# Windowed attention with an RWKV channel mix on one core: the second half of each early group's exponentials goes through GpSimd, one long ScalarE exponential and VectorE, and the written order of the opening is a new one

## The chip, the cores and the metric

The kernel runs on one core of one Trainium2 chip. The metric is device microseconds of one execution of the whole program, weights and inputs loaded from HBM, result written back to it. All data are float32 at the kernel's edges.

## The reference

Attention over 8 batches, 8 heads, 576 positions and 64 values per head, in which a position sees itself and the 63 before it; its output is the input `x` (512 columns) of an RWKV channel mix with a hidden width of 1024.

```python
scores = np.matmul(q, k.transpose(0, 1, 3, 2)) / np.sqrt(D)
mask = (rel >= 0) & (rel < 64)                 # rel = row - column
scores = np.where(mask, scores, -1e9)
scores = scores - np.max(scores, axis=-1, keepdims=True)
attn = np.exp(scores)
attn = attn / (np.sum(attn, axis=-1, keepdims=True) + 1e-09)
x = np.matmul(attn, v)                         # heads side by side: B, S, 512

x_prev = np.concatenate([zeros, x[:, :-1]], axis=1)
xk = mu_k * x + (1.0 - mu_k) * x_prev
xr = mu_r * x + (1.0 - mu_r) * x_prev
k = np.maximum(xk @ w_k, 0.0)                  # 512 x 1024
v = k * k @ w_v                                # 1024 x 512
r = 1.0 / (1.0 + np.exp(-(xr @ w_r)))          # 512 x 512
return r * v
```

## The kernel before

The 4608 positions are cut into nine units of 512. A unit's attention is done by groups: one group is a pair of heads over one unit, four groups to a unit, 36 groups. The first eight groups (two units), called whole, work on blocks of 128 key columns; the later ones work on narrower bands of 32 rows, and are turned by VectorE.

A whole group `g` goes through these steps. `whole_scores` (TensorE) fills two PSUM banks, one for each head, `h` = 0 and 1, from `qk`, the queries and keys of the group; the queries and keys of groups 2 and 3 lie in a buffer named `qks`. For each head, `soften` then makes four blocks of 128 columns. For each block, `least` (VectorE, with its read of an accumulator) writes the negated, masked scores to `pr` and their smallest to `nmax`, and `exp` (ScalarE, followed by a read of an accumulator) takes the exponential of the block, with `nmax` as its bias and the row sum as second output. When all eight blocks of both heads are done, `shares` (two short VectorE instructions) makes the reciprocals `rs`, and `scale`, once for each head and over 512 columns, multiplies `pr` by them on GpSimd or VectorE. `flip` transposes the four blocks of a head on TensorE against `ident`; a copy on ScalarE or VectorE brings them from PSUM to `pt`. `whole_values` (TensorE, needs `v`) multiplies, a copy brings the result to `xT`, and a few elementwise steps on ScalarE, GpSimd and VectorE mix it with the position before into `xm`. The products of `xm` with the weights follow.

The weights come in as raw blocks of 512 KB (`raw`, from `w_r`, `w_k`, `w_v`), and each half of a block is decoded once: a sign on ScalarE (`wt<-raw`), a clamp on GpSimd or VectorE (`wt<-wt`), then three VectorE steps that need a PSUM bank for a while and end in `whole`. The first products use `whole` in float32 (`xm,whole`); the later ones use `ws`, the weight split in two parts by a cast and a subtraction, three instructions for a product (`xs,ws` and `ks,ws`).

Each piece of work is recorded with a helper, so that nearly all instructions carry that helper's line, L160 before and L161 after. `ORDER` is a table that writes out, for each engine, the order of the first 1700 or so pieces by their numbers; a piece waits until all that it needs is done, and whatever stands behind it on its engine waits with it. `play` places the rest. The queue `SP` issues all the loads in the order of its own list. `values`, the counterpart of `whole_values` for the banded groups, begins every pair of groups with an instruction that fills TensorE's instruction stream with empty instructions up to a given place in a window of 128 instructions:

```python
            tc.keep_in_program_order(nc.tensor.addr_align(128, offset=ALIGN))
```

`ALIGN` is 102. The number of empty instructions that it makes depends on how many instructions of TensorE stand ahead of it.

Of the kernel before, what the change touches and what calls it, by code (L numbers as in the profile page):

```python
# [13 lines left out]
AF = mybir.ActivationFunctionType  # L14
ALU = mybir.AluOpType
PSUM = bass.MemoryType.PSUM

P = 128
# [5 lines left out]
G = 4  # L24
# [26 lines left out]
USTEPS = 40  # L51


PAIRED = 8

WHOLES = 8
# [12 lines left out]
FAR_LINK = 45  # L69

ALIGN = 102

RING = 8

# [1 line left out]

ORDER = {
# [11 lines left out]
    ),  # L89
    "DVE": (  # L90
# [13 lines left out]
    ),  # L104
    "ACT": (
# [12 lines left out]
    ),  # L118
    "POOL": (
# [4 lines left out]
    ),  # L124
# [8 lines left out]
    ),  # L133
}
# [7 lines left out]
def attn_rwkv_kernel(ctx, tc, qT, kT, v2, mu_k, mu_r, w_k, w_v, w_r, out):  # L142
    nc = tc.nc
# [18 lines left out]
    pe, dve, sca, pool, dma = (Engine(e) for e in (nc.tensor, nc.vector, nc.scalar, nc.gpsimd, nc.sync))  # L162
# [120 lines left out]
    def d1(n):  # L283
        return 65 + 1.04 * n
# [4 lines left out]
    def act_ns(n):  # L289
        return 5 + 0.92 * n  # L290
# [10 lines left out]
    engines = {"DVE": dve, "POOL": pool}  # L301

    def bank(*shape):
        return psum.tile([P, *shape], F32, name="bank")
# [78 lines left out]
    words, whole, pairs, rooms = {}, {}, {}, {}  # L383
# [177 lines left out]
            arrived["v", g] = [transfer(lambda e, x=x: load_whole(e, *x), 4 * P * P * (x[3] - x[2]), held["v", g], key=key)  # L561
                               for x in whole_loads[u]]

    banks, weights, sums, flipped = {}, {}, {}, {}
    xTs, got = {}, {}
    chain = {}

# [9 lines left out]
                          k[hr, k0:k0 + P], start=True, stop=True)  # L577

    def flip(g, h):
        ps = flipped[g, h] = bank(G, P)  # L580
        for e in range(G):
            pe.transpose(ps[:, e, :], weights[g, h][:, e, :], ident)
# [118 lines left out]
    def soften(g, h, p, own):  # L701
        u, _ = groups[g]
        key = p.key + 0.5
# [5 lines left out]
        rows = Hold("pr")  # L709
        if h == 0:  # L710
            chain[g, "sums"], chain[g, "exps"] = Hold("sums"), []
        exps, begin = chain[g, "exps"], None
        for o in range(G):
            def least(e, o=o):
                if o == 0:
                    pr = at.tile([P, G * P], F32, name="pr", bufs=4)
                    weights[g, h] = pr[:, :G * wide].rearrange("p (i k) -> p i k", k=wide)
                    if g not in sums:
                        sums[g] = [at.tile([P, 2, G], F32, name=nm, bufs=4) for nm in ("nmax", "sums", "rs")]
                if whole:  # L720
                    starts = [(u * UB + 2 * o + j) % NB for j in range(2)]
                    mask = masks[starts.index(0) if 0 in starts else None]
                else:
                    mask = banded[first.get(o)]
                dve.tensor_tensor_reduce(weights[g, h][:, o], banks[g][h][:, o], mask,
                                         scale=-SCALE, scalar=FAR, op0=ALU.add, op1=ALU.min,
                                         accum_out=sums[g][0][:, h, o:o + 1])

            def exp(e, o=o):
                pr = weights[g, h]  # L730
                sca.activation(pr[:, o], pr[:, o], AF.Exp, bias=sums[g][0][:, h, o:o + 1], scale=-1.0,
                               accum_out=sums[g][1][:, h, o:o + 1])

            takes = [rows, chain[g, "sums"]] if o == 0 else []
            q = Piece("DVE", key, 211 if whole else 180, least, [p, begin, chain.get("masks")], takes, own)
            begin = begin or q
            exps.append(Piece("ACT", key, 385 if whole else 356, exp, [q]))
            chain["least"] = q
        chain[g, h, "pr"] = rows
        if h == 0:  # L740
            return
# [346 lines left out]
```

## Time and profile before

| what | value |
|---|---|
| median of three runs | 624.54 us (624.25, 624.54, 627.5) |
| the profiled execution, its time | 623.52 us |
| the profiled execution, its span | 621.7 us |
| granted TensorE clock, mean | 0.999 of full speed |
| TensorE products, busy | 603.0 us, 97% of the span |
| VectorE, busy | 399.7 us, 64% |
| ScalarE, busy | 372.8 us, 60% |
| GpSimd, busy | 118.7 us, 19% |
| read from HBM, written to it | 45.09 MB, 9.44 MB |

The span runs from the first to the last instruction of the profiled execution; the time of the execution is 1.8 us longer. Busy shares are over the whole span, and PE stands for TensorE's products, PEld for its weight loads, DVE for VectorE, ACT for ScalarE, POOL for GpSimd, SP for the queue of the loads. A row of a timeline gives start and length in microseconds, and in brackets how long the engine was idle ahead of it and what ended that.

### The profile page before, as it was taken

The page shows a single profiled execution, that of the slowest core. Times are in us where ns is not written, and L with a number is a line of the kernel's source. Part 1 is how long each engine was busy: PE and PEld are TensorE (multiplying, and loading weights), DVE is VectorE, ACT ScalarE, POOL GpSimd, SP SyncE. Part 2 cuts the span into 40 slices and gives each one's busy share as a digit, 9 for nine tenths or more (in the row PEclk, how much of TensorE's full clock was granted, in tenths as well). Part 3 has the DMA queues.
Part 4 walks back from the last instruction along what each step waited for, and adds up shares of the span by engine and source line. Part 5 has one row for each costly group of instructions (what it writes and reads, how often), then busy time and mean ns, then how long its engine had stood idle before and what let it go on. Part 6 is the DMA issues. An engine that isn't in the chain of part 4 may idle for free.

```text
span 621.7 us, 18051 instructions
## 1 busy us (share of the span) xinstructions
PE 603.0 (97%) x7168; PEld 474.2 (76%) x7168; DVE 399.7 (64%) x1218; ACT 372.8 (60%) x1058; POOL 118.7 (19%) x189
## 2 busy tenths in 40 slices
PE   2999999989999999999999999999999999999997
PEld 2655478878888888888888888888888888888885
DVE  5999998766685468636872778276837684665211
ACT  5989975558356735763575448564757466734630
POOL 6551532311210122011300330023002200111000
PEclk9999999999999999999999999999999999999999
DMA  8995213313231223123222322133212231010001
GB/s 309 363 322 163 96 28 100 107 34 92 68 115 35 78 76 107 43 65 94 84 74 53 105 88 74 53 90 102 76 53 90 77 100 28 1 53 18 0 18 51
DMA packets 58866, 55.70 MB, mean 90 GB/s; under 512 B 10144, under 2 KB 52128, under 8 KB 58784
## 3 DMA queue, kind: packets, MB, share of 16 engines
q1 hardware_dynamic: 58784, 54.56, 28.2%
q8 instruction: 57, 0.93, 0.7%
q14 instruction: 25, 0.20, 0.1%
HBM read 45.09 MB, written 9.44 MB: 88 GB/s over the span
## 4 chain that ended last, share of the span: by engine, by line
PE 95%; DVE 2%; DMA 1%; issue 1%; SPq 0%; POOL 0%; ACT 0%; DVEq 0%
PE bank L160 95%; DMA raw<-w_r 1%; DVE pr L160 1%; SPq L160 0%; DVE bank L160 0%; DVE xm L160 0%; POOL pr L160 0%; DVE mu L160 0%; DVE r L160 0%; ACT wt L160 0%; POOL wt L160 0%; DVE whole L160 0%; DVE rs L160 0%; DVE nmax L160 0%; DVEq L160 0%
## 5 line engine op out<-in xcount | busy, mean ns | idle before, releaser
L160 PE MATMUL bank<-xs,ws 128*128 128x512 f32 x1152 | 273.0, 396 | 0.0
L160 PEld LDWEIGHTS bank<-xs,ws 128*128 128x128 f32 x1152 | 215.8, 188 | 51.2
L160 PE MATMUL bank<-ks,ws 128*128 128x512 f32 x864 | 206.2, 397 | 0.0
L160 PEld LDWEIGHTS bank<-ks,ws 128*128 128x128 f32 x864 | 161.4, 188 | 38.8 <-issue 0.5
L160 DVE TENSOR_TENSOR ks<-kf,ks 128x512 fp32r<-128x512 f32 x71 | 51.7, 730 | 105.1 <-ACT ks L160 105.1
L160 ACT ACTIVATE pr<-pr,nmax 128x96 f32<-128x96 f32 (+1 forms) x288 | 105.9, 371 | 10.1 <-DVE nmax L160 9.6
L160 ACT ACTIVATE kf<-bank 128x512 f32<-128x512 f32 x72 | 42.9, 598 | 64.9 <-PE bank L160 64.9
L160 POOL CAST ks<-kf 128x512 fp32r<-128x512 f32 x10 | 6.1, 610 | 266.3 <-ACT kf L160 266.3
L160 ACT COPY xT<-bank 128x256 f32<-128x256 f32 (+1 forms) x35 | 13.2, 419 | 72.1 <-PE bank L160 72.1
L160 ACT ACTIVATION_READ_ACCUMULATOR pr<-pr,nmax 128x1 f32 x288 | 54.6, 190 | 0.0
L160 DVE CUSTOM_DVE_ANT_0 pr<-bank,bands 128x96 f32<-128x96 f32 x224 | 42.6, 249 | 14.1 <-PE bank L160 14.1
L160 PEld LDWEIGHTS bank<-pt,v 32*64 32x64 f32 (+1 forms) x2912 | 39.2, 131 | 9.6 <-issue 7.5
L160 ACT ACTIVATE kf<-kf 128x512 f32<-128x512 f32 x71 | 44.7, 632 | 2.1
L160 PE MATMUL bank<-pt,v 32*64 32x64 f32 (+3 forms) x2912 | 42.1, 235 | 2.4 <-issue 2.0
L160 ACT ACTIVATE th<-bank 128x512 f32<-128x512 f32 x36 | 21.3, 592 | 38.0 <-PE bank L160 27.5
L160 DVE SCALAR_TENSOR_TENSOR r<-bank,r 128x512 f32<-128x512 f32 x36 | 24.5, 680 | 30.1 <-PE bank L160 30.1
L160 PE MATMUL bank<-xm,whole 128*128 128x512 f32 x96 | 42.4, 594 | 0.5 <-DVE xm L160 0.5
L160 ACT CAST ks<-kf 128x512 fp32r<-128x512 f32 x62 | 38.4, 620 | 2.5 <-POOL kf L160 0.7
L160 PE MATMUL bank<-qk 64*32 64x96 f32 (+1 forms) x1984 | 33.4, 256 | 6.6 <-DMA qk<-kT 6.6
L160 PEld LDWEIGHTS bank<-qk 64*32 64x32 f32 (+1 forms) x1984 | 28.6, 110 | 13.9 <-DMA qk<-qT 7.0
L160 ACT CAST xs<-d 128x512 fp32r<-128x512 f32 x51 | 30.6, 615 | 13.6 <-POOL d L160 11.5
L160 DVE TENSOR_TENSOR xs<-d,xs 128x512 fp32r<-128x512 f32 x57 | 36.4, 681 | 0.1
(82 smaller groups left out, 546.7 us busy)
## 6 DMA issues: line engine op xcount, KB each, us to landing
v<-v SPq DMA_DIRECT2D x116, 64.0 KB, 2.1
raw<-w_k SPq DMA_DIRECT2D x8, 512.0 KB, 7.1
raw<-w_v SPq DMA_DIRECT2D x8, 512.0 KB, 4.9
v<-v SPq DMA_DIRECT2D x112, 32.0 KB, 1.8
v<-v SPq DMA_DIRECT2D x11, 192.0 KB, 5.2
raw<-w_r SPq DMA_DIRECT2D x4, 512.0 KB, 6.5
outT<-r SPq DMA_DIRECT2D x8, 256.0 KB, 2.0
qk<-qT SPq DMA_DIRECT2D x8, 224.0 KB, 3.6
```

The lines of the kernel that those rows point to most:

```text
L160: return lambda *args, **kw: tc.keep_in_program_order(op(*args, **kw))
```

## The change

For the second head (`h` = 1) of each of the eight whole groups, the four exponentials of 128 columns are replaced by three pieces: `above` subtracts `nmax` from the 512 columns of `pr` (on GpSimd in seven groups and on VectorE in one, by the table), `exp_all` is one ScalarE exponential over 512 columns without bias and without sums, and `total` is a VectorE reduction that makes the four sums. The first head keeps its four exponentials. The tables in `ORDER` are replaced for all five engines. Ahead of the first `flip`, a second instruction of the filling kind, with `START` = 69, goes into TensorE's stream.

```diff
+SPREAD = {(g, 1) for g in range(8)}
 ALIGN = 102
+START = 69
 ORDER = {
     "PE": (
-        507, 531, 529, 560, 527, 553, 555, 551, 584, 557, 580, 687, 582, 1481, 1488, 1495, 1482, 1489, 608,
+        507, 530, 558, 528, 526, 553, 581, 551, 549, 555, 577, 579, 681, 1473, 1480, 1487, 1474, 1488, 604,
...
     def flip(g, h):
+        if not turned:
+
+            turned.append(tc.keep_in_program_order(nc.tensor.addr_align(128, offset=START)))
         ps = flipped[g, h] = bank(G, P)
...
-        exps, begin = chain[g, "exps"], None
+        exps, begin, leasts = chain[g, "exps"], None, []
...
-            exps.append(Piece("ACT", key, 385 if whole else 356, exp, [q]))
+            if (g, h) in SPREAD:
+                leasts.append(q)
+            else:
+                exps.append(Piece("ACT", key, 385 if whole else 356, exp, [q]))
             chain["least"] = q
+
+        def above(e):
+            pr = weights[g, h]
+            engines[e].tensor_sub(pr, pr, sums[g][0][:, h].unsqueeze(2).to_broadcast([P, G, wide]))
+
+        def exp_all(e):
+            pr = weights[g, h]
+            sca.activation(pr, pr, AF.Exp, scale=-1.0)
+
+        def total(e):
+            engines[e].tensor_reduce(sums[g][1][:, h], weights[g, h], axis=mybir.AxisListType.X, op=ALU.add)
+
+        if (g, h) in SPREAD:
+            q = Piece({"POOL": 1000, "DVE": d1(G * wide)}, key, 0, above, leasts, port=True)
+            q = Piece("ACT", key, act_ns(G * wide) + 20, exp_all, [q])
+            exps.append(Piece("DVE", key, d1(G * wide), total, [q]))
```

TensorE's rows up to the first products of `xm` with a weight, before. The groups come in turn: scores (`qk`, `qks`), flips (`ident,pr`, four to a head) and values (`pt,v`); the scores of groups 0 and 1 stand together in the first row, those of groups 2 and 3 are the two rows with `qks`.

```order
L160 MATMUL bank<-qk 64x128 x32
L160 MATMUL bank<-ident,pr 128x128 x4
L160 MATMUL bank<-qks 64x128 x16
L160 MATMUL bank<-ident,pr 128x128 x8
L160 MATMUL bank<-pt,v 64x64 x16
L160 MATMUL bank<-ident,pr 128x128 x4
L160 MATMUL bank<-qks 64x128 x16
L160 MATMUL bank<-pt,v 64x64 x16
L160 MATMUL bank<-ident,pr 128x128 x4
L160 MATMUL bank<-qk 64x128 x16
L160 MATMUL bank<-ident,pr 128x128 x4
L160 MATMUL bank<-xm,whole 128x512 x5
```

The same place of TensorE's stream in the changed kernel; the row of L583 is the new filling instruction.

```order
L161 MATMUL bank<-qk 64x128 x32
L161 MATMUL bank<-qks 64x128 x16
L583 ISA
L161 MATMUL bank<-ident,pr 128x128 x8
L161 MATMUL bank<-pt,v 64x64 x16
L161 MATMUL bank<-qks 64x128 x16
L161 MATMUL bank<-ident,pr 128x128 x8
L161 MATMUL bank<-pt,v 64x64 x16
L161 MATMUL bank<-ident,pr 128x128 x8
L161 MATMUL bank<-qk 64x128 x16
L161 MATMUL bank<-xm,whole 128x512 x5
```

The work ahead of the first `xm` product is the same (80 scores, 24 flips, 32 values), but the scores of group 2 now stand ahead of the first flip, and those of group 3 behind the values of group 0.

The loads issued by SP, from its third to its twelfth row before, down to the queries of group 2 (the last row). `128x1024` is a raw block of 512 KB, `128x512` is 256 KB.

```order
L160 DMA raw_146<-w_r 128x1024
L160 DMA qk<-qT 128x512
L160 DMA qk<-kT 128x512
L160 DMA raw_151<-w_r 128x1024
L160 DMA raw_153<-w_k 128x1024
L160 DMA raw_155<-w_r 128x1024
L160 DMA qk<-qT 128x448
L160 DMA muk<-mu_k 128x4
L160 DMA qks<-kT 128x512
L160 DMA qks<-qT 128x512
```

The same queue after, from the third row (one load of keys and one of queries stand ahead, as before) to the fourteenth, again down to the queries of group 2.

```order
L161 DMA mur<-mu_r 128x4
L161 DMA qk<-qT 128x512
L161 DMA raw_149<-w_r 128x1024
L161 DMA raw_151<-w_r 128x1024
L161 DMA qk<-kT 128x512
L161 DMA raw_154<-w_k 128x1024
L161 DMA muk<-mu_k 128x4
L161 DMA v<-v 128x384
L161 DMA qks<-kT 128x512
L161 DMA raw_179<-w_r 128x1024
L161 DMA qk<-qT 128x448
L161 DMA qks<-qT 128x512
```

The keys of group 1 now stand behind two raw blocks where one stood ahead of them, and the queries of group 2 stand behind a first load of `v` as well. Behind these rows come three raw blocks, three loads of `v` and, in the 24th and 26th row, the keys and queries of group 3.

ScalarE's rows in the changed kernel from the last exponentials of group 1 to the second copy `xT`; `COPY pt` follows the flips, `COPY xT` the values, `pr<-pr 128x512` is the new long exponential, and the four short ones in one row belong to group 2.

```order
L161 ACTIVATE pr,sums<-pr,nmax 128x128
L161 COPY pt<-bank 128x512
L161 ACTIVATE pr,sums<-pr,nmax 128x128
L161 COPY pt<-bank 128x512
L161 ACTIVATE pr<-pr 128x512
L161 CAST ws_384<-whole 128x512
L161 COPY xT<-bank 128x512
L161 ACTIVATE pr,sums<-pr,nmax 128x128 x4
L161 CAST ws_427<-whole 128x512
L161 COPY pt<-bank 128x512 x2
```

The last of the four short exponentials of group 1 now stands between the two copies of group 0's flips.

## Rows read from the trace of the kernel before

**Rows 1.** TensorE in order of time: start, length, engine, line, operation and number of instructions, and in brackets the idle time ahead of it and what ended it. The stretch to the first product of `xm`, and two later places.

```profile
4.19 1.98 PE L160 MATMUL bank<-qk 64*64 64x128 f32 x32 [4.19 <-DMA qk<-kT]
8.61 1.98 PE L160 MATMUL bank<-qk 64*64 64x128 f32 x32 [2.44 <-DMA qk<-kT]
15.20 1.11 PE L160 MATMUL bank<-ident,pr 128*128 128x128 f32 x4 [4.61 <-POOL pr L160]
...
18.16 1.94 PE L160 MATMUL bank<-ident,pr 128*128 128x128 f32 x8
...
21.70 1.10 PE L160 MATMUL bank<-qks 64*64 64x128 f32 x32
...
23.60 1.15 PE L160 MATMUL bank<-pt,v 128*64 128x64 f32 x30 [0.15 <-ACT pt L160]
...
27.43 4.53 PE L160 MATMUL bank<-xm,whole 128*128 128x512 f32 x10 [0.48 <-DVE xm L160]
...
68.17 0.63 PE L160 MATMUL bank<-ident,pr 128*128 128x128 f32 x4 [0.83 <-issue]
...
123.12 5.27 PE L160 MATMUL bank<-xs,ws 128*128 128x512 f32 x22
130.38 0.80 PE L160 MATMUL bank<-pt,v 32*64 32x96 f32 x45 [1.98 <-issue]
```

**Rows 2.** Busy time by stretch: from and to, length, then busy us and instructions of PE, PEld, DVE, ACT and POOL, the granted TensorE clock, the DMA engines' busy share and GB/s.

```profile
0.00:20.00 20.00, 8.76 (x108) 7.09 (x108) 11.47 (x55) 12.21 (x43) 12.96 (x37) 1.00 0.92 321
20.00:40.00 20.00, 19.06 (x264) 12.57 (x264) 19.29 (x76) 19.55 (x68) 11.00 (x16) 1.00 0.97 337
```

**Rows 3.** The empty instructions of the filling in `values` (L610), by source line, at the first and at the second place where it stands: number, length, first and last start.

```profile
L610 PEldq NOP  x84: 13/13/13, 124.1 to 130.2; - x84
```

```profile
L610 PEldq NOP  x10: 13/13/13, 158.6 to 159.3; - x10
```

**Rows 4.** Three loads on the SP queue, in order of time: start and length of the issue.

```profile
3.05 0.43 SPq L160 DMA_DIRECT2D raw<-w_r  x1
...
7.86 0.33 SPq L160 DMA_DIRECT2D qks<-qT  x1
...
13.32 0.33 SPq L160 DMA_DIRECT2D qks<-qT  x1
```

**Rows 5.** The same three loads in the view of the transfers: KB, and us from issue to landing.

```profile
raw<-w_r SPq DMA_DIRECT2D x1, 512.0 KB, 6.7
...
qks<-qT SPq DMA_DIRECT2D x1, 256.0 KB, 6.8
...
qks<-qT SPq DMA_DIRECT2D x1, 256.0 KB, 4.6
```

**Rows 6.** Groups of instructions by operation and shape: number, busy us and mean ns of one, idle time ahead of them and what ended it.

```profile
L160 ACT ACTIVATE pr<-pr,nmax 128x128 f32<-128x128 f32 x64 | 25.1, 398 | 1.8 <-DVE nmax L160 1.8
L160 ACT ACTIVATION_READ_ACCUMULATOR pr<-pr,nmax 128x1 f32 x288 | 54.6, 190 | 0.0
L160 ACT ACTIVATE kf<-kf 128x512 f32<-128x512 f32 x71 | 44.7, 632 | 2.1
L160 POOL TENSOR_TENSOR pr<-pr,rs 128x512 f32<-128x512 f32 x11 | 12.0, 1100 | 18.4 <-ACT kf L160 8.7 <-ACT ws L160 3.5 <-DVE nmax L160 2.9
L160 DVE TENSOR_TENSOR pr<-pr,rs 128x512 f32<-128x512 f32 x5 | 4.4, 871 | 0.0
```

**Rows 7.** Single steps in order of time, of GpSimd, ScalarE and VectorE, in the opening.

```profile
14.11 2.04 POOL L160 TENSOR_TENSOR pr<-pr,rs 128x512 f32<-128x512 f32 x2
```

```profile
16.99 0.56 ACT L160 COPY pt<-bank 128x512 f32<-128x512 f32 x1
...
22.12 0.39 ACT L160 ACTIVATE pr<-pr,nmax 128x128 f32<-128x128 f32 x1
...
24.90 0.57 ACT L160 COPY xT<-bank 128x512 f32<-128x512 f32 x1
```

```profile
22.63 0.17 DVE L160 TENSOR_SCALAR rs<-sums 128x8 f32<-128x8 f32 x1
22.83 0.20 DVE L160 RECIPROCAL rs<-rs 128x8 f32<-128x8 f32 x1
...
25.52 0.68 DVE L160 SCALAR_TENSOR_TENSOR bank<-raw,bank 128x512 uint32<-128x512 uint32 x1
26.13 1.16 DVE L160 SCALAR_TENSOR_TENSOR xm<-xT,mur,xm 128x512 f32<-128x512 f32 x1
```

**Rows 8.** The same mixing step of ScalarE and of VectorE at a later place.

```profile
38.23 0.72 ACT L160 ACTIVATE xm<-xT,mu 128x512 f32<-128x512 f32 x1
```

```profile
37.69 0.75 DVE L160 SCALAR_TENSOR_TENSOR xm<-xT,mur,xm 128x512 f32<-128x512 f32 x1
```

**Rows 9.** ScalarE in order of time ahead of the idle time of TensorE that ends at 68.17.

```profile
65.24 0.68 ACT L160 ACTIVATE wt<-raw 128x512 f32<-128x512 f32 x1 [1.39 <-DMA raw<-w_v]
...
67.50 0.56 ACT L160 COPY pt<-bank 128x512 f32<-128x512 f32 x1
```

**Rows 10.** One VectorE operation of one shape at two places, and the GpSimd instruction at the second.

```profile
38.95 0.42 DVE L160 TENSOR_SCALAR wt<-wt 128x512 uint32<-128x512 uint32 x1
```

```profile
62.77 1.26 DVE L160 TENSOR_SCALAR wt<-wt 128x512 uint32<-128x512 uint32 x1
```

```profile
62.47 1.28 POOL L160 TENSOR_TENSOR pr<-pr,rs 128x512 f32<-128x512 f32 x1 [3.49 <-ACT ws L160]
```

More of the change, by code (lines that the diff above doesn't have):

```diff
@@ L562, in load_v @@
                                for x in whole_loads[u]]
-    banks, weights, sums, flipped = {}, {}, {}, {}
+    banks, weights, sums, flipped, turned = {}, {}, {}, {}, []
     xTs, got = {}, {}
```

86 rows, old and new, of the table ORDER are left out of this document.

## The prediction

> **What bounds the kernel now.** I read the busy shares first: TensorE is at work in 603.0 of 621.7 us, so a change counts only where it moves TensorE's idle time, or the part that TensorE runs at half speed. Its timeline says where the rest lies [rows 1]: 4.19, 2.44 and 4.61 us ahead of scores and flips of the opening, 0.15 and 0.48 ahead of values and the first `xm` product at 27.43, and after that two gaps alone, 0.83 at 68.17 and 1.98 at 130.38. So the opening ends at 27.43; what comes later is a chain of products without a hole, and each microsecond by which the first `xm` product moves is a microsecond of the result, as long as no later gap opens or closes. The clock is the second thing to see there: 32 matmul instructions of scores take 1.98 us at 8.61 and 1.10 at 21.70, of one shape, so TensorE ran at the lower of its two levels in the first 20 us though the clock column prints 1.00 [rows 1, 2]. Third, the stretches: between 20 and 40 ScalarE is busy 19.55 of 20 us and VectorE 19.29, and the DMA engines 97% [rows 2]. Three resources are full there, and the change relieves one and loads another.
>
> **The new operations.** Beside TensorE: four short exponentials with their reads (398 and 190 ns, which start 0.39 apart, so 1.55 us) become one of 512 columns, which I price by a ScalarE instruction of that shape, 632 ns [rows 6]: 0.9 us less for a group, 7.4 for eight. GpSimd gets seven subtractions of the shape of its scaling, 1.10 us each, VectorE one of 0.87 [rows 6]. VectorE's reductions are not in this trace; a 512-column instruction there takes from 0.42 to 0.87 [rows 10, 6], I take the decode's 0.68 [rows 7], 5.5 us for eight, on an engine that is as full as ScalarE. None of it is on TensorE; it counts through the opening's chain.
>
> **The fillings.** This is the part that I read as dearest. The first filling in `values` made 84 empty instructions from 124.1 to 130.2, 73 ns apart, the second 10 from 158.6 to 159.3, 78 apart [rows 3]. They go through TensorE's sequencer while products queued earlier still run: these ended at 128.39 [rows 1], some 4.3 us after the first empty one, and the remaining time is the gap of 1.98. Both numbers follow from counting the stream: a float32 product issues four instructions, a transpose or a part of a split product two, and waits count. 2004 instructions stand ahead of the first filling; 84 of filling to place 102 puts it at 18 of 128, so the count starts at 62. From there 886 instructions lead to the second: 102 + 886 is 92 modulo 128, and 10 are missing, as the row has. In the changed kernel 198 instructions stand ahead of the new filling: 62 + 198 is 4, and 65 are missing to 69. At 73 ns that is 4.7 us, between the scores of group 2 and the first flip, with at most one group of scores (1.98) queued to hide it. To the first filling of `values` it is then 1801 more, place 78, 24 fillers, 1.75 us, less than the 4.3 that were queued there: the gap of 1.98 goes.
> [...]
>
> **The opening.** Landings first. The raw block issued at 3.05 landed after 6.7, at 9.75, when 2048 KB had been asked for; the queries of group 2, issued at 7.86, at 14.66 (3810 KB); those of group 3, issued at 13.32, at 17.92 (5090 KB) [rows 4, 5]. That is some 393 KB a microsecond. In the new order the queries of group 2 are complete at 4000 KB, about 15.1; the second load of `v` for group 0 at 6080 KB, 20.4; the queries of group 3 at 7070 KB, 23.0, 5 us later than before.
> TensorE now goes in this order. The scores of group 2 can start at 15.1, and all must be issued before the filling: from 0 to 1.98 us, I take 0.5. The filling ends at 20.3. Eight flips at the lower speed take 1.9 [rows 1], to 22.2. ScalarE then copies one head (0.57), does the exponential that stands between (0.39 to 0.48), and copies the other (0.57) [rows 7]: 23.9. Values of group 0, 1.1: 25.0. Scores of group 3 fall behind that.
> Group 1 is later still. Its last exponential is the one between the copies, which ends at 23.4; the two short instructions of `shares` stand behind two decode steps that need a bank freed by the first copy (23.0 + 2 x 0.68, then 0.17 + 0.20): 25.2, with small delays between engines. Two scalings on GpSimd (2.04): 27.3. Flips at the full speed, to 27.9. Their copies stand behind four exponentials of group 2 and a cast, which hold ScalarE to 28.1: 29.2. Values (1.15): 30.3. Then the copy to `xT` (0.57), ScalarE's mixing step (0.72) and VectorE's (1.16 in the opening, 0.75 later) [rows 7, 8], the last behind a decode step: 33.0 to 34.2. I take 34.2, since 1.16 is the row of this place.
> So the first `xm` product moves from 27.43 to 34.2: +6.8. Against it −1.98 for the filling and −0.83 for the gap at 68.17, where ScalarE's copy was late behind a sign step that had waited 1.39 us for a block of `w_v` [rows 9]; in the new SP list the first block of `w_v` comes earlier (34th row, 37th before). Sum +4.0. The profiled execution, 623.52, would be 627.5; it lies 1.0 below the median, and from the median it gives 628.5.
>
> **Rivals.** *The filling is hidden or cheap in the opening.* TensorE waits there anyway: without the 65 the flips could start when GpSimd has scaled group 0, about 17.4. The next limits are the landings (20.4 for `v`, 23.0 for the queries of group 3): scores to 24.1, flips of group 1 to 25.2, copies 26.4, values 27.5, mixing 2.7 to 3.2, first `xm` about 30.7. That is +3.3 − 2.8 = +0.5, 625.0, no change that a measurement of this kernel tells (0.5%, 3.1 us). For it: all the trace's empty instructions stood behind a full queue of products, so their 73 ns may be another thing than in an empty one. Against: the last ones of the 84 came after the queue had run dry.
> *Faster.* ScalarE is what holds the opening, and loses 0.95 us in each of the four groups ahead of the first `xm` product: it comes near 23.3 instead of 27.43, and with −2.8 the time is 617.6. It decides from a first `xm` product before 27.1, where −0.3 and −2.8 make 3.1. For it the 19.55 of 20 us [rows 2]; against it, that the loads (97% of their time) are later for groups 2 and 3, and that ScalarE is only one link.
> *Slower by another way, the filling apart.* GpSimd and VectorE get in each other's way: a VectorE step takes 0.42 us at 38.95 and 1.26 at 62.77, beside a GpSimd multiply of 1.28, of which two take 2.04 elsewhere [rows 10, 7]. Seven more such multiplies at up to 0.8 for each, some half of them on the path, add 2.8 to the forecast: 631.3.
> [...]
>
> **Numbers.** The forecast, first `xm` at 32 to 35, has 0.42 (627 to 630; 0.05 of it within 0.5%); the hidden filling 0.35, all within 0.5%; ScalarE as the holder 0.15, faster; contention on top 0.08, slower. Together faster 0.15, same 0.40, slower 0.45. The predicted time is 628.5. The range leaves out the lower half of the fast case and the end of the contention: 621.5 to 631.8.
>
> **What would show it.** Right: 65 empty instructions at L583 some 4.7 us long, and the first flip right behind them near 20.3; 24 at the first filling of `values` and no gap there; the first `xm` product at 34, the gap at 68 gone. Wrong: the empty instructions 20 ns apart, or over before the scaling of group 0; the first flip near 17.4 or the first `xm` near 30; a landing of the queries of group 2 or 3 away from 15.1 and 23.0 by more than 1 us; VectorE's reductions above 0.87; a new gap in the chain after 34, which the sum takes to be without one.

## The result: 629.11 us, slower by the forecast's size, and the profile after

| | before | after |
|---|---|---|
| median | 624.54 us (five runs here, 624.25 to 627.5) | 629.11 us (five runs, 628.28 to 629.35) |
| profiled execution, its span | 621.7 us | 627.5 us |
| ratio | | 1.0059, 95% interval 1.004 to 1.0078 |

The ratio is worked out from all runs; the two medians alone give 1.0073, inside its interval. The forecast was 628.5, slower, with 621.5 to 631.8 as its range. TensorE's timeline after shows where the time came from; the columns are those of [rows 1].

```profile
10.24 1.99 PE L161 MATMUL bank<-qk 64*64 64x128 f32 x32 [3.67 <-DMA qk<-kT]
15.65 1.99 PE L161 MATMUL bank<-qks 64*64 64x128 f32 x32 [3.43 <-DMA qks<-qT]
21.20 1.94 PE L161 MATMUL bank<-ident,pr 128*128 128x128 f32 x8 [3.56 <-POOL wt L161]
...
24.68 1.97 PE L161 MATMUL bank<-pt,v 128*64 128x64 f32 x30 [0.39 <-ACT pt L161]
26.58 1.99 PE L161 MATMUL bank<-qks 64*64 64x128 f32 x32
28.50 1.97 PE L161 MATMUL bank<-ident,pr 128*128 128x128 f32 x8
...
31.63 1.15 PE L161 MATMUL bank<-pt,v 128*64 128x64 f32 x30 [0.16 <-ACT pt L161]
...
35.07 4.56 PE L161 MATMUL bank<-xm,whole 128*128 128x512 f32 x10 [0.24 <-DVE xm L161]
```

The first `xm` product starts at 35.07, where it started at 27.43 [rows 1]. Values, scores and flips from 24.68 to 30.5 still take 1.97 to 1.99 us, half speed (the values at 31.63 took 1.15); before, full speed began by 21.70, with scores in 1.10 [rows 1]. The 3.56 ahead of the first flip is put down to GpSimd's `wt`, which has nothing to do with a flip. What stood there is seen in the view of the filling's source line:

```profile
L583 PEldq NOP  x65: 13/13/13, 16.1 to 21.0; - x65
```

```profile
L614 PEldq NOP  x24: 13/13/13, 131.0 to 132.7; - x24
```

65 and 24 empty instructions, as counted, at 4.9/64 = 77 ns for the first. The gaps at 68 and at 130 [rows 1] are both gone; one small one is new:

```profile
558.60 0.82 PE L161 MATMUL bank<-pt,v 32*64 32x32 f32 x53 [0.20 <-issue]
```

Busy time on the two sides of the first `xm` product (columns as in [rows 2]), before and after:

```profile
0.00:27.43 27.43, 15.25 (x248) 12.31 (x249) 18.87 (x88) 19.64 (x72) 17.31 (x43) 1.00 0.95 342
27.43:622.00 594.57, 587.71 (x6920) 461.85 (x6920) 380.82 (x1131) 353.13 (x987) 101.39 (x147) 1.00 0.26 78
```

```profile
0.00:35.07 35.07, 17.69 (x249) 14.56 (x249) 22.58 (x96) 19.59 (x51) 24.25 (x49) 1.00 0.93 318
35.07:628.00 592.93, 588.48 (x6920) 461.99 (x6920) 379.22 (x1127) 350.79 (x960) 101.85 (x145) 1.00 0.25 75
```

TensorE does the same work in the opening. It is idle 17.38 us there for 12.18 (+5.20) and at work 17.69 for 15.25 (+2.44, the half speed that lasts longer). Behind it, up to the end of the span (the windows shown end 0.3 and 0.5 us later), it is at work 0.77 longer, and idle 2.61 less (−0.83, −1.98, +0.20). The sum, 5.80, is the difference of the spans.

### The profile page after: what moved, and what is told of

It is laid out like the page before. It is cut to its first block, busy times and chain, and to the rows that moved or that the text cites. A ratio compares the mean times of both kernels' runs of the same rounds, so it can differ in the third digit from the quotient of the medians.

```text
span 627.5 us, 18008 instructions
## 1 busy us (share of the span) xinstructions
PE 606.2 (97%) x7168; PEld 476.5 (76%) x7168; DVE 401.8 (64%) x1222; ACT 370.4 (59%) x1009; POOL 126.1 (20%) x194
## 3 DMA queue, kind: packets, MB, share of 16 engines
q1 hardware_dynamic: 58784, 54.56, 28.2%
## 4 chain that ended last, share of the span: by engine, by line
PE 95%; DMA 1%; SPq 1%; POOL 1%; DVE 1%; ACT 0%; issue 0%; DVEq 0%
PE bank L161 95%; DMA raw<-w_r 1%; SPq L161 1%; POOL pr L161 0%; POOL wt L161 0%; DVE pr L161 0%; POOL ws L161 0%; ACT pt L161 0%; DVE bank L161 0%; DVE xm L161 0%; DVE r L161 0%; ACT wt L161 0%; DVE whole L161 0%; ACT pr L161 0%; DVE rs L161 0%
## 5 line engine op out<-in xcount | busy, mean ns | idle before, releaser
L161 ACT ACTIVATE pr<-pr,nmax 128x96 f32<-128x96 f32 (+1 forms) x256 | 93.4, 367 | 8.8 <-DVE nmax L161 8.0
L161 ACT ACTIVATION_READ_ACCUMULATOR pr<-pr,nmax 128x1 f32 x256 | 48.2, 188 | 0.0
L161 PE MATMUL bank<-pt,v 32*64 32x64 f32 (+3 forms) x2912 | 43.6, 236 | 2.1 <-ACT pt L161 1.9
L161 DVE TENSOR_TENSOR xs<-d,xs 128x512 fp32r<-128x512 f32 x60 | 39.4, 700 | 1.3 <-POOL xs L161 0.8
```

The costliest lines, as they stand in the source:

```text
L161: return lambda *args, **kw: tc.keep_in_program_order(op(*args, **kw))
```

## The experiments

All times are medians of four to six runs; ratios are to the kernel before, run on the same chip beside them.

**Without the new filling.** The later place is moved along, so that the first filling in `values` keeps 24 empty instructions.

```diff
-ALIGN = 102
+ALIGN = 37
-            turned.append(tc.keep_in_program_order(nc.tensor.addr_align(128, offset=START)))
+            turned.append(None)
```

> The changed kernel without its new filling; the place of the later fillings is moved by as much, so that the first one in `values` has 24 empty instructions as in the changed kernel. If the 65 hold the opening (my theory), the first flip starts at the end of its scaling on GpSimd, about 17.7 instead of 21.2; after that the queries of group 3, which landed at 24.7 in the changed kernel, are the next limit, the flips of group 1 end 3 us earlier, the first product of xm comes near 32, and the time is about 626. If the filling hides behind waits that are there anyway, the first xm product stays at 35 and the time at 629. If the loss was the filling alone, with nothing else later than before, the time falls by the whole 4.9 us, to 624.

651.81 us, ratio 1.0429 (1.0413 to 1.0444). The opening did what was expected; TensorE's timeline, opening first and then two of seven gaps far behind it:

```profile
17.42 1.66 PE L161 MATMUL bank<-ident,pr 128*128 128x128 f32 x8
...
23.71 1.10 PE L161 MATMUL bank<-qks 64*64 64x128 f32 x32 [1.84 <-DMA qks<-qT]
...
30.78 1.09 PE L161 MATMUL bank<-qk 64*64 64x128 f32 x28 [1.25 <-DMA qk<-kT]
31.80 4.56 PE L161 MATMUL bank<-xm,whole 128*128 128x512 f32 x10
...
168.39 0.64 PE L161 MATMUL bank<-pt,v 32*64 32x96 f32 x20 [1.63 <-issue]
...
580.14 0.50 PE L161 MATMUL bank<-pt,v 32*64 32x96 f32 x21 [1.66 <-issue]
```

The first flip came 3.8 us earlier, the first `xm` product 3.3. What held that product last was a load: the scores of group 4, which stand ahead of it, waited for their keys until 30.78. But in every second pair of banded groups the values now stop for 1.6 to 1.9 us, 20 products ahead of their end. That is no term of any theory of mine, and it hides the total.

**Before, with another place.**

```diff
-ALIGN = 102
+ALIGN = 42
```

> The kernel before with 42 for 102 as the place of the fillings in `values`: 24 empty instructions instead of 84 at the first of them, 10 and 9 at the later ones as before. If the gap of 1.98 us at 130.38 is the sequencer's time for 84 empty instructions, it goes, and the time falls by 2.0, to 622.5. If the gap has another cause (a wait that no row shows), or if the place 102 itself matters, the time stays at 624.5 or rises.

644.11 us, 1.0304 (1.028 to 1.0327). The gap at 130 is gone, and the same stops appear (first and last of seven rows, the first with the products behind it, and one stretch of 100 us):

```profile
163.87 0.63 PE L160 MATMUL bank<-pt,v 32*64 32x96 f32 x22 [1.66 <-issue]
164.43 10.05 PE L160 MATMUL bank<-ks,ws 128*128 128x512 f32 x36
...
572.95 0.51 PE L160 MATMUL bank<-pt,v 32*64 32x96 f32 x23 [1.39 <-issue]
```

```profile
300.00:400.00 100.00, 97.98 (x1148) 79.20 (x1149) 65.25 (x207) 58.73 (x170) 16.70 (x26) 0.97 0.26 74
```

The seven stops add to 10.9 us, and the granted clock, 0.97 in such a stretch and 1.00 before, shows that products run slow for a while: the 36 behind the first stop took 279 ns each, where 60 of the same shape took 14.27 us, 238 each, at 145.79. In all, TensorE is at work for 616.4 us here and for 603.0 before, which is the rest. So the fillings are not padding to be made small: they set the place in the stream at which the values stand.

**Before, with a filling of 65 ahead of its first flip,** and the place 107, which leaves 24 to fill in `values`.

```diff
-ALIGN = 102
+ALIGN = 107
+START = 4
     def flip(g, h):
+        if not turned:
+            turned.append(tc.keep_in_program_order(nc.tensor.addr_align(128, offset=START)))
```

> The kernel before with a filling of 65 empty instructions ahead of its first flip, as the changed kernel has one, and 24 at the first filling of `values`. There the first flip waits for GpSimd until 15.2, and the scores ahead of it end at 10.6. If a filling costs only what no wait covers, 65 end near 15 and cost nothing: the time is that of the kernel with the place 42, 622.5. If a filling costs its length wherever it stands, 4.9 more: 627.4.

621.6 us, 0.9943 (0.993 to 0.9957): faster than both kernels.

```profile
L582 PEldq NOP  x65: 13/13/13, 8.9 to 13.6; - x65
```

```profile
15.06 1.11 PE L161 MATMUL bank<-ident,pr 128*128 128x128 f32 x4 [4.64 <-POOL pr L161]
...
27.17 4.53 PE L161 MATMUL bank<-xm,whole 128*128 128x512 f32 x10 [0.25 <-DVE xm L161]
```

The filling ends 1.4 us ahead of the flip that waits for GpSimd: it cost nothing here, where it was covered (first flip at 15.06 for 15.20). The gap at 130 is gone, the stops are not there at the place 107, and the gap at 68 is gone too in this run.

**Transposes in place of the empty instructions.**

```diff
-            turned.append(tc.keep_in_program_order(nc.tensor.addr_align(128, offset=START)))
+            turned.append(None)
...
+        if len(turned) == 1:
+            turned.append(None)
+            for _ in range(15):
+                pe.transpose(ps[:, 0, :], ident, ident)
```

With `ALIGN` = 68:

> The changed kernel with 15 transposes of the unit matrix in place of the 65 empty instructions, which are overwritten by the flip that follows (24 at the first filling of `values`, as there). At the lower speed they last 15 x 0.243 = 3.6 us, so the first flip stays near 21.2. In the changed kernel values, scores and flips from 24.7 to 30.5 ran at half speed, 1.97, 1.99 and 1.97 us where 1.15, 1.10 and 1.09 are the other speed. If TensorE's idle time in the filling kept it slow, these run at full speed and the first xm product comes 2 to 2.6 us earlier: 626.5 to 627. If the clock goes by the time since the start or by something else, all stays at 629.

649.38 us, 1.0383 (1.0356 to 1.0409), with stops of 1.2 to 1.8 us again. With `ALIGN` = 102:

> The changed kernel with 15 transposes of the unit matrix in place of the 65 empty instructions, as once before, but with the place 102 in `values` (58 empty instructions at the first filling there, 4.2 us, which the products queued ahead just cover). There the first xm product came at 33.77 for 35.07, with full speed from 20 on. If the place is all that made that run 20 us longer, it is now 1.3 us below the changed kernel, 627.8. If the transposes or the later places cost more, 630 or above.

628.34 us, 1.007 (1.0049 to 1.0091). Two kernels that differ by 34 empty instructions ahead of the values lie 21 us apart: that is the place alone. Their openings are alike; the timeline of the second:

```profile
17.16 3.46 PE L161 MATMUL bank<-ident 128*128 128x128 f32 x15
20.42 1.17 PE L161 MATMUL bank<-ident,pr 128*128 128x128 f32 x8
...
33.66 4.56 PE L161 MATMUL bank<-xm,whole 128*128 128x512 f32 x10
```

With the transposes in the filling's place the flips ran at nearly full speed (1.17 us for 1.94; 1.09 later), and the first `xm` product came 1.4 earlier; here too the scores of group 4 ahead of it waited for their keys, until 32.64. In the medians that is 0.8 us, less than they tell apart.

**Without the new filling, at the place 102** (89 to fill at the first values).

> The changed kernel without its new filling, and with the place 102 kept in `values`: the first filling there has 89 empty instructions, the later places are those of the changed kernel. If the 19 to 25 us lost with the places 37, 42 and 68 come from the place in the stream alone, they are gone here. The opening gains 3.3 us as without the filling (first xm product at 31.8), and 89 empty instructions at 73 ns, 6.5 us, are 2.2 more than the 4.3 of products that are queued: 629.1 - 3.3 + 2.2 = 628.0, with a gap of about 2 us at the first values of a banded group. If the new filling does anything else for the later part, 640 or more.

630.3 us, 1.0091 (1.0068 to 1.0113).

```profile
28.47 1.15 PE L161 MATMUL bank<-pt,v 128*64 128x64 f32 x30 [0.16 <-ACT pt L161]
...
32.29 1.09 PE L161 MATMUL bank<-qk 64*64 64x128 f32 x28 [1.28 <-DMA qk<-kT]
33.31 4.56 PE L161 MATMUL bank<-xm,whole 128*128 128x512 f32 x10
```

```profile
135.97 3.60 PE L161 MATMUL bank<-pt,v 32*64 32x96 f32 x192 [2.32 <-issue]
```

The stops are gone, so the new filling does nothing else for the later part. The gap is 2.32, as worked out; that the values behind it took 3.60 us, for 2.41 in the changed kernel, was not in the sum. Its first 60 us are instruction for instruction those of the first experiment, and yet the first `xm` product came at 33.31 for 31.80. Two things differ between the two executions, which ran on two chips: full speed came by 28.5 here (the eight flips at 25.42 still took 1.89 us) and by 19 there (the eight flips at 17.42 took 1.66 us, the values at 20.71 then 1.15), and the keys of group 4, for which the scores ahead of that product waited in both, were there at 32.29 here and at 30.78 there. The last link is the keys, 1.51 us apart.

**The changed kernel once more.**

> The changed kernel once more, with a second profile, to see how much of its opening differs from execution to execution. If it is fixed by the program, the first xm product comes within 0.5 us of 35.07 and the time is 629.1. If the clock's rise and the landings scatter, the products of the opening change from half to full speed elsewhere than at 31, and the first xm product lies up to 2 us away.

628.53 us, 1.0064 (1.0052 to 1.0077); first flip at 20.86, first `xm` product:

```profile
34.61 4.56 PE L161 MATMUL bank<-xm,whole 128*128 128x512 f32 x10 [0.23 <-DVE xm L161]
```

This opening repeats to half a microsecond.

**The filling moved ahead of the scores of group 1.**

```diff
-START = 69
+START = 67
     def whole_scores(g):
+        if g == 1:
+            tc.keep_in_program_order(nc.tensor.addr_align(128, offset=START))
```

> The changed kernel with the same filling of 65 empty instructions ahead of the scores of group 1 in place of the first flip; everything behind the first flip stands at the same place of the instruction stream as in the changed kernel. TensorE waits there for the keys of group 1 until 10.2. If the filling costs only what no wait covers, it runs from about 5 to 10 and costs nothing: first flip at 17.4, first xm product at 31.8 as without it, and, the places in `values` being those of the changed kernel, no gaps there: 629.1 - 3.3 = 625.8. If a filling costs its length anywhere, the scores of group 1 start near 15 and the time stays at 629 or more.

628.61 us, 1.0071 (1.0047 to 1.0094). The expected 3.3 us did not come.

```profile
L571 PEldq NOP  x65: 13/13/13, 4.7 to 9.4; - x65
```

```profile
18.10 2.12 PE L161 MATMUL bank<-ident,pr 128*128 128x128 f32 x8
22.81 1.97 PE L161 MATMUL bank<-pt,v 128*64 128x64 f32 x32 [2.60 <-DVE nmax L161]
...
32.20 1.97 PE L161 MATMUL bank<-ident,pr 128*128 128x128 f32 x8
...
35.59 4.56 PE L161 MATMUL bank<-xm,whole 128*128 128x512 f32 x10
```

The first flip is 3.1 earlier than in the changed kernel, and all of it is lost again. The values of group 0 wait until 22.81; the second load of `v`, issued at 15.24, took 7.4 us to land, 22.6, where it took 6.1 in the changed kernel, so the named `nmax` is not what they waited for. And TensorE stayed at half speed to 34. Taking the filling out of the chain was worth nothing here, where the next two things were as late.

**The old operations in the new order** (on top of the moved filling): `above` and `total` issue nothing, and

```diff
         def exp_all(e):
             pr = weights[g, h]
-            sca.activation(pr, pr, AF.Exp, scale=-1.0)
+            for o in range(G):
+                sca.activation(pr[:, o], pr[:, o], AF.Exp, bias=sums[g][0][:, h, o:o + 1], scale=-1.0,
+                               accum_out=sums[g][1][:, h, o:o + 1])
```

> The kernel with the moved filling, and the four short exponentials with their sums back in the place of the one long exponential; nothing is subtracted on GpSimd and nothing summed on VectorE. The written order is otherwise that of the changed kernel. ScalarE has 0.9 us more to do in a group. If landings, the filling and the written order hold the opening (my theory), the first xm product moves by at most 1 us either way: 625 to 627 where the new operations give 625.8. If ScalarE holds it, four groups at 0.9 make 629.5. If GpSimd's subtractions were themselves on the path at 1.0 each, 623 or less.

629.2 us, 1.0076 (1.0053 to 1.0099), first `xm` product at 35.48 for 35.59. In this order the new operations neither win nor lose.

**The new operations in the order of before** (on top of its filling of 65): GpSimd subtracts with the last of the four `least`, the long exponential stands at the last of the four, the sum ahead of `shares`.

> The order of before with its filling moved ahead of the first flip (621.6 us) and the new operations in it: for the second head of each of the eight groups GpSimd subtracts when the last of the four least values is there, one long exponential stands where the last of four stood, and VectorE sums ahead of `shares`. If the opening of before is held by loads and by the chain of its first group, that chain gets 0.8 longer (1.04 + 0.63 + 0.69 for 1.55) and ScalarE's relief gives part of it back: 621.6 to 622.6. If ScalarE holds it, three groups at 0.9 are won: 618.8. If GpSimd and VectorE get in each other's way, 624 or more.

628.04 us, 1.0059 (1.004 to 1.0078), 6.4 us above the kernel that it is built on. ScalarE, GpSimd, VectorE and TensorE in turn:

```profile
22.48 0.63 ACT L161 ACTIVATE pr<-pr 128x512 f32<-128x512 f32 x1 [1.77 <-POOL pr L161]
```

```profile
27.04 1.04 POOL L161 TENSOR_TENSOR pr<-pr,nmax 128x512 f32<-128x512 f32 x1 [0.48 <-ACT pr L161]
28.18 1.36 POOL L161 TENSOR_SCALAR xm<-xT,mu 128x512 f32<-128x512 f32 x2
```

```profile
28.91 1.17 DVE L161 SCALAR_TENSOR_TENSOR xm<-xT,mur,xm 128x512 f32<-128x512 f32 x1 [1.43 <-POOL xm L161]
```

```profile
30.22 4.53 PE L161 MATMUL bank<-xm,whole 128*128 128x512 f32 x10 [2.37 <-DVE xm L161]
...
50.82 1.09 PE L161 MATMUL bank<-ident,pr 128*128 128x128 f32 x8 [0.93 <-POOL pr L161]
```

ScalarE waits for the subtraction, and the next subtraction stands ahead of GpSimd's mixing step, for which VectorE and then TensorE wait: 3.05 us in the opening, and some 3 more in five small gaps behind it. The rival's place was right (GpSimd), its mechanism was not: the steps are not slower (1.17 us for VectorE's, 1.16 in [rows 7]), they queue. This prices the operations at this place in GpSimd's queue; no other place was tried.

**Earlier loads** (on top of the moved filling): `v` of group 0 and the keys and queries of group 3 ahead of a raw block.

```diff
     "SP": (
-        ... 677, 23, 43, 51, 83, 13, 674, 611, 12, 614, 676, 39, 24, 40, 612, ...
+        ... 677, 23, 43, 51, 13, 12, 39, 40, 83, 674, 611, 614, 676, 24, 612, ...
```

> The kernel with the moved filling (628.6), in which SP issues the loads of v for group 0 and the keys and queries of group 3 ahead of the third raw block that stands there, in place of behind it and two more small loads: the queries of group 3 are complete after 5986 KB for 7074, 2.8 us earlier by the rate of 393 KB a microsecond, v for group 0 1.5 us earlier. If these landings hold the opening now that the filling is out of the way, scores of group 3 start near 22.5 for 25.3, the first xm product comes 2 to 2.5 us earlier, and the time is 626.5. If ScalarE, the flips or the clock hold it, or the raw block that now lands 2.4 us later does, the time stays at 628.6 or rises.

629.88 us, 1.008 (1.0062 to 1.0098), with runs from 627.47 to 631.15; no gain in the median. The profile is of the fastest of these runs, and there the first `xm` product came 2.0 us earlier than with the moved filling alone (35.59), as expected.

```profile
23.97 1.62 PE L161 MATMUL bank<-qks 64*64 64x128 f32 x32
...
32.53 1.09 PE L161 MATMUL bank<-qk 64*64 64x128 f32 x28 [1.99 <-DMA qk<-kT]
33.55 4.56 PE L161 MATMUL bank<-xm,whole 128*128 128x512 f32 x10
```

The scores of group 3 no longer wait. The scores of group 4, ahead of the first `xm` product in the table, then do, for a block of keys that lands near 32.5. It is the 32nd row of the SP list, behind three more raw blocks.

**Before with its filling of 65, and GpSimd's scalings of group 0 ahead of a clamp.**

```diff
     "POOL": (
-        747, 4, 16, 28, 526, 525, 53,
+        747, 4, 16, 526, 525, 28, 53,
```

> The order of before with the filling ahead of its first flip (621.6), and on GpSimd the two scalings of group 0 ahead of one clamp that stood before them. TensorE waits 4.6 us for these scalings, so the first flip comes 0.6 to 1 us earlier. If that wait is on the path to the first xm product, the time is 620.6 to 621. If ScalarE and the loads hold what follows, it stays at 621.6; if the decode behind the later clamp is needed first, 622 or more.

621.39 us, 0.9948 (0.9933 to 0.9963), the same as without. Its profiled execution was its slowest, 622.6, and there the first `xm` product came at 29.69, with half speed to 26 (scores at 24.20 in 1.99 us, at 27.91 in 1.10): the order of before knows a late clock too.

## Why the prediction was right, point by point

- **The fillings** were right in number (65, 24) and pitch (77 and 74 ns for 73), and so was the gap that goes. No run shows the 20 ns that the prediction names as a sign of being wrong.
- **What the filling is worth on the path** was read a little high. The prediction's two cases, 34.2 and 30.7 for the first `xm` product, put 3.5 us on it. It delays the first flip by some 3.5 us. Without it, the first `xm` product came at 31.80 and 33.31, with it at 35.07 and 34.61, so 1.3 to 3.3 of the 7.64 us hang on it; and without it 89 empty instructions stand at the values, which took back more than that (630.3 for 628.5 to 629.1, a difference that the intervals do not quite settle). The moved filling, which covered it, gained nothing.
- **The landings** were later than forecast: the scores of group 2 started at 15.65 for a landing at 15.1, `v` was there at 21.0 for 20.4, the queries of group 3 at 24.7 for 23.0, which is more than the 1 us that the prediction itself named as a sign of being wrong. The mis-sized term is the rate. 393 KB a microsecond is the rate between the last two of the three landings in [rows 4] and [rows 5]; all three give 372, and here the 3070 KB from the queries of group 2, complete at 15.5, to those of group 3 took 9.2 us, 334 a microsecond. The keys of group 4 were missing from my chain. In five runs the scores ahead of the first `xm` product waited for them, to between 30.78 and 32.75, and the product followed a microsecond later, at 31.80 to 33.77, which is why the second case of my list, 30.7 and 625.0, was not reached by any kernel in this order.
- **The clock** was the step that failed. "Flips at the full speed, to 27.9" ended at 30.47. GpSimd's scalings ahead of them ended at 28.2 for 27.3, which is 0.9 of it. The rest goes with half speed: the values of group 0, the scores of group 3 and these flips stand one behind the other and took 1.97 to 1.99 us each, where full speed takes 1.09 to 1.15. TensorE ran at half speed ten microseconds longer than before (full speed by 31.63, before by 21.70), 2.44 us more of work in the opening.

```profile
26.19 2.04 POOL L161 TENSOR_TENSOR pr<-pr,rs 128x512 f32<-128x512 f32 x2 [0.80 <-DVE rs L161]
```

- **The end came out by luck.** The values of group 1 ended at 32.8 for 30.3, 2.5 us late, and yet the first `xm` product came at 35.07 for 34.2. The prediction's own terms behind 30.3 (0.57, 0.72, a decode step of 0.68, then 0.75 or 1.16) give 33.0 or 33.4, and its second case counts the same steps as 2.7 to 3.2; 34.2 comes out only as 33.0 plus 1.16, with VectorE's mixing step in it twice. Without that slip the forecast would have been some 0.8 lower, 627.7, and the first `xm` product 1.7 late. In the run these steps took 2.3 us: the mixing step took 0.74, not 1.16, and the decode step ahead of it ran beside ScalarE's.

```profile
33.67 0.69 DVE L161 TENSOR_SCALAR bank<-wt 128x512 uint32<-128x512 uint32 x1
34.27 0.74 DVE L161 SCALAR_TENSOR_TENSOR xm<-xT,mur,xm 128x512 f32<-128x512 f32 x1
```

- **The two gaps** went as worked out, −0.83 and −1.98. The first is not steady: with the loads in the order of before some 0.4 is left for it at the place 42 (11.3 us in eight such gaps, of which the seven stops are 10.9), and it was absent with the filling of 65. So some of the 0.83 was one execution's. The sum of +4.0 lacked 0.77 of slower products and 0.20 of a new gap behind the opening (0.79 when the changed kernel ran once more); 7.64 for 6.8 is the rest. The profiled execution moved by 5.8, the medians by 4.6.
- **ScalarE as the holder** has a small slip in its price: 27.43 less four times 0.95 is 23.6, not 23.3, which makes its time 617.9.
- **The operations** are priced right by the rows (GpSimd 1081 ns, VectorE's reduction 681, ScalarE's exponential 630):

```profile
L161 POOL TENSOR_TENSOR pr<-pr,nmax 128x512 f32<-128x512 f32 x7 | 7.6, 1081 | 5.7 <-DVE nmax L161 3.5 <-PE bank L161 2.2
L161 DVE TENSOR_REDUCE sums<-pr 128x4 f32<-128x512 f32 x8 | 5.4, 681 | 1.6 <-ACT pr L161 1.5
L161 ACT ACTIVATE pr<-pr 128x512 f32<-128x512 f32 x8 | 5.0, 630 | 2.7 <-POOL pr L161 2.7
```

That ScalarE holds the opening of this order is refuted: with 0.9 us more in a group the first `xm` product stayed. It is the new written order, its loads among it, that makes the changed kernel slower: with the old operations, a covered filling and no large stop in either, it took 629.2 us (1.0076) and the order of before 621.6 (0.9943), and the first `xm` product stands at 35.48 and 27.17. Which part of the order does it is not settled: earlier loads for group 3 alone won nothing in the median, those for group 4 were not tried, and how much of the half speed follows from the order stays open, since the same opening showed an early and a late rise (by 19 and by 28.5).

## What to carry to other kernels

Empty instructions cost their time here only where no wait covered them (65 under a wait of 4.64 us cost nothing, 84 behind 4.3 us of products left a gap of 1.98), so count them from the stream and put them under the longest wait; a gain in one link counted only up to the next landing (first flip 3.1 us earlier, first `xm` product 0.5 later), which has to be looked for all the way to the product that ends the stretch. An operation moved to an idle engine was not free there (3.05 us at the first `xm` product in the order of before): ask what stands behind it in that engine's queue, in each order apart. And never change the count of instructions ahead of a place-sensitive stretch without looking for stops in it (seven here, 10.9 us at the place 42).

## What the runs showed of the hardware that was not expected

- **The place of the values in TensorE's stream decided some 20 us** (651.81 us for 630.3, 649.38 for 628.34, 644.11 for 624.91). At the places 37, 42 and 68 there are seven stops of 1.2 to 1.9 us, and slower products behind; at 102 and 107 there is at most one, near 558, of 0.2 to 0.8 us. The seven come once in two pairs of groups; from pair to pair there are 886 or 887 instructions and 10 or 9 to fill, 896, so the stops stand 1792 instructions apart. What they are was not tested, and why only every second pair has one and why 102 escapes them is open.
- **Half speed lasted some ten microseconds longer in one execution than in another with the same opening.** Two executions of the same first 60 us, on two chips, reached full speed by 19 and by 28.5 (eight flips in 1.66 us at 17.42 in the one and in 1.89 at 25.42 in the other). What that is worth at the first `xm` product (31.80 and 33.31) is not shown, since in both it came behind scores that waited for the keys of group 4.
